# Column halves evicted from tiles of their own, doubled reads, and other layouts for staged weights

## The chip, the cores and the metric

The kernel runs on one core of one Trainium2 chip. Its time is device microseconds (us) from the launch to the end of the last transfer; three runs of the kernel before gave 1161.09 to 1162.67, median 1161.89. A profiled execution is a run of its own, and stands beside these. Engine names are those of the profile: PE (matrix products; PEld its weight loads), DVE, ACT, POOL, SP. DMA transfers are issued by SP (hardware queue q1), a few by ACT (q10), and the adding ones by POOL (software queue q0); all share the core's 16 DMA engines. DMA shares in the profile are means over these 16.

## The reference

Input `x` is 2048 tokens of 576 values, float32. With `xn` its layer norm over the 576 values,

```
out = x + attention(xn @ wqkv) @ wo + relu(xn @ w1) @ w2
```

The attention has 32 heads of 18 values; token s looks at the eight tokens s, s-2, ..., s-14 (those before the start are masked). `w1` is 576 x 4608, `w2` 4608 x 576, `wqkv` 576 x 1728, `wo` 576 x 576. All of it is float32 in and out.

## The kernel before

**Operands.** Each float32 operand of a product is cut in two: a high part, rounded by a copy on ACT, and a low part, the difference, formed on DVE or (for splits marked `pooled`) on POOL (`two`, L170 to L177). A product is then the sum of high x high, high x low and low x high. The 576 rows of a contraction are four pieces of 128 and a last piece of 64. Since a piece of 64 rows fills half of the 128 partitions, it is loaded twice, into partitions 0 to 63 and 64 to 127 (`for part in LOW, UPP`), one DMA for each half.

**Phases.** The tokens are done in two phases `ph` of 1024: eight row blocks of 128, in pairs `tb` of 256 columns of transposed `xn`. In each phase the first six of the 36 column tiles of `w1` (128 columns each) go through plain loops (slots `n`: `h_two` for the hidden layer, `o_two` for its product with `w2`). The other 30 go in 15 pairs `p` by a seven-product (Strassen) scheme: for each pair two groups `g`, one for each two pairs of row blocks; `group` (L1176) runs eight steps, each with a piece of hidden layer, one with `w2` (`o_half`), and one or more evictions.

**The attention** is done in four units `u` of 8 heads (144 columns). The q, k, v products of units 1 to 3 are put into groups 5, 11 and 17 and the group after each; their weights are loaded three groups earlier (`wq_load`, in step 4 of that group, right behind `sw_load` of the next `w1` pair) and split in steps of the next two groups (`wq_split`). The rest of a unit is vector work in a list `bg`, which `run_bg` fills in wherever a small model of DVE's clock (`room`, `DUE`) says that it fits ahead of the next thing that PE waits for.

**Evictions.** A finished PSUM tile is 256 tokens by a column half (`CUT`: 256 or 320 columns). `evict` (L707) copies it on ACT into half of a tile `ev` of 2 x 576 columns; when both halves are there, POOL issues one adding DMA (read the output in HBM, add, write) for each row block of 128 rows, 2304 bytes a row. The pool has two such tiles, so a copy waits until the transfers out of the tile used two pairs earlier have landed. The products with `wo` go the same way, in transfers of 4 x 32 rows. Only the very first sums (phase 0, first three tiles) add `x` on DVE and are stored by SP.

**Queues.** Each engine works in the order in which the code wrote its instructions. SP issues its DMAs in that order too: one that waits for a buffer holds back the ones behind it. SP runs ahead of PE as far as free buffers allow. The pair's `w1` columns come by `sw_load` (L894): four DMAs of two 128 x 128 blocks (512 bytes a row) and two for the last 64 rows; POOL forms sums of them (`sw_mix`), ACT and DVE split them (`sw_prep`).

**Between phases** (the seam) SP writes the attention's transposed output to HBM (`o_out`, L616, eight DMAs a unit), reads it back by token quarters (`ot_in`, by `words_in`, L393), and reads the next phase's transposed `xn` (`xt_in`, also by `words_in`, from `words`). `wo` is staged in HBM and read at the end of a phase (`wo_load`, L254).

Of the kernel before, what the change touches and what calls it, by code (L numbers as in the profile page):

```python
# [26 lines left out]
NU = 4  # L27
# [43 lines left out]
def tile_body(ctx: ExitStack, tc: tile.TileContext, x, wqkv, wo, w1, w2, out):  # L71
# [37 lines left out]
    f32 = lambda ap: ap.bitcast(F32)  # L109

# [74 lines left out]
    def w1_load(ph, c, f):  # L185
# [6 lines left out]
        for part in LOW, UPP:  # L192
            nc.sync.dma_start(st[part, 512:640], w1[KT * P : D, cs])
# [24 lines left out]
    def wq_load(ph, u):  # L218
# [7 lines left out]
        for kt in range(KT + 1):  # L226
            v = z[:, kt, :].rearrange("p (s c) -> p s c", s=3)
            if kt < KT:
                nc.sync.dma_start(v, wq_src[kt * P : (kt + 1) * P, :, c])
            else:  # L230
                for part in LOW, UPP:
                    nc.sync.dma_start(v[part], wq_src[KT * P : D, :, c])
# [310 lines left out]
    def attention(ph, u):  # L543
# [9 lines left out]
        if u == 0:  # L553
            OD[ph] = odp.tile([D, 4, 2 * P], F32, name="od")
# [106 lines left out]
    def ot_in(ph, r):  # L661
# [5 lines left out]
        words_in(f32(lo), OD[ph][:, r])  # L667
# [38 lines left out]

    def evict(ph, tb, h, z, what):  # L707
        key = ph, tb, what
        if key not in EV:
            EV[key] = evp.tile([P, 2, D], F32, name="ev"), []  # L710
        acc, done = EV[key]
        cols = CUT[h]
        nc.scalar.activation(acc[:, :, cols], z[:, :, 0 : cols.stop - cols.start], AF.Copy)  # L713
        done.append(h)
        if len(done) == 2:
            del EV[key]
            for k in range(2):
                if what == "wo":
# [863 lines left out]
```

## Time and profile before

| | |
|---|---|
| median of three runs | 1161.89 us |
| profiled execution, its time | 1158.69 us |
| its span, first to last instruction | 1156.9 us |
| granted clock of PE, mean | 0.994 |
| DMA packets, data | 159811, 176.82 MB |
| DMAs issued by POOL that add (ev and pr) | 276 of 288 KB |

The page cuts the span into 40 slices of 28.9 us with the busy tenths of each engine. A row of the waits names the engine and line that waited, what ended the wait, the total, how often, and the longest. A row of the timeline gives start, duration, engine, line, operation and tiles, and in brackets the idle time just before it with what ended it. A row of the windows gives the stretch, its length, the busy time of each engine with instructions in brackets, the granted clock, the mean busy share of the 16 DMA engines (waiting inside a packet counts, so it can pass 1), and GB/s.

### The profile page before, as it was taken

Reading aid. Unit: us, or ns where it says so; the run is one execution under the profiler, and the core shown is the slowest. Engines: PE = TensorE matmul, PEld = TensorE weight load, DVE = VectorE, ACT = ScalarE, POOL = GpSimd, SP = SyncE. Lnnn points to the kernel's source line nnn. Section 1 sums busy time; section 2 is a strip of 40 time slices with the busy share of each in tenths; the row PEclk is TensorE's granted clock in tenths of the full one; section 3 lists DMA queues with packets and bytes.
Section 4 is the critical chain, followed back from the end, with each engine's and each line's share of the span. In section 5 each row is a group of like instructions: output and inputs, shape, how many; then the busy total and the mean of one; then the engine's idle time right before and its main releaser. Section 6 shows DMA issues by size and latency. Waiting matters only on the chain.

```text
span 1156.9 us, 38381 instructions
## 1 busy us (share of the span) xinstructions
PE 1116.8 (97%) x16410; PEld 1094.4 (95%) x16410; DVE 814.3 (70%) x1249; ACT 560.3 (48%) x1348; POOL 469.5 (41%) x514
## 2 busy tenths in 40 slices
PE   8999999999999999997999999999999999999896
PEld 8999999999999989997999999999999999999895
DVE  7676889699688677964317248868897896888521
ACT  4444464454454455564534345535545544555540
POOL 2324552453353345553322235435524523555331
PEclk9999999999999999998999999999999999999998
DMA  7469985795786687899947258759848957888984
GB/s 219 153 160 218 189 157 93 157 202 89 162 179 122 136 168 140 145 193 267 180 71 164 43 122 171 126 104 191 160 85 179 194 91 170 144 155 141 236 125 112
DMA packets 159811, 176.82 MB, mean 153 GB/s; under 512 B 36233, under 2 KB 107145, under 8 KB 159609
## 3 DMA queue, kind: packets, MB, share of 16 engines
q0 software_dynamic: 44352, 81.45, 46.8%
q1 hardware_dynamic: 114604, 92.03, 27.3%
q8 instruction: 129, 2.11, 0.7%
q10 hardware_dynamic: 684, 0.88, 0.2%
q14 instruction: 42, 0.34, 0.1%
HBM read 74.07 MB, written 95.70 MB: 147 GB/s over the span
## 4 chain that ended last, share of the span: by engine, by line
PE 74%; DMA 10%; DVE 5%; ACT 4%; issue 3%; POOL 1%; SPq 1%; ACTq 0%; DVEq 0%; POOLq 0%
PE po L163 23%; PE po L142 19%; PE ph L163 12%; PE pm L163 9%; PE pm L142 5%; DMA out<-ev 4%; PE ph L142 3%; DMA att<-od 2%; ACT ev L713 1%; PE ph L130 1%; DVE ar L759 1%; DVE ar L176 1%; PE po L130 1%; DVE wq L176 1%; DMA xS<-out 1%
## 5 line engine op out<-in xcount | busy, mean ns | idle before, releaser
L163 PE MATMUL po<-ar 64*128 64x320 f32 (+1 forms) x5760 | 469.2, 291 | 1.5 <-ACT ev L713 1.0
L163 PEld LDWEIGHTS po<-ar 64*128 64x128 f32 x5760 | 410.3, 185 | 4.1 <-ACT ev L713 1.6
L726 POOL DMA_DIRECT2D out<-ev x256 | 226.2, 1024 | 386.6 <-ACT ev L713 346.7
L163 PE MATMUL ph<-xT,ar 64*128 64x256 f32 x2520 | 323.5, 277 | 10.0 <-ACT pm L977 7.2
L163 PEld LDWEIGHTS ph<-xT,ar 64*128 64x128 f32 x2520 | 287.4, 185 | 15.5 <-ACT pm L977 10.3
L713 ACT ACTIVATE ev<-po 128x512 f32<-128x512 f32 (+1 forms) x266 | 171.5, 650 | 219.1 <-PE po L163 95.9
L163 PE MATMUL pm<-xS,ar 64*128 64x256 f32 x2160 | 261.1, 276 | 1.3 <-ACT u L981 0.6
L163 PEld LDWEIGHTS pm<-xS,ar 64*128 64x128 f32 x2160 | 236.9, 184 | 2.9 <-ACT u L981 1.3
L176 DVE TENSOR_TENSOR ar<-st,ar 128x256 fp32r<-128x256 f32 (+3 forms) x232 | 148.8, 646 | 87.5 <-ACT ar L172 76.4
L174 POOL TENSOR_TENSOR ar<-st,ar 128x256 fp32r<-128x256 f32 (+1 forms) x72 | 95.8, 1335 | 160.5 <-ACT ar L172 157.6
L172 ACT ACTIVATE ar<-st 128x256 fp32r<-128x256 f32 (+3 forms) x304 | 148.6, 503 | 15.2 <-DMA st<-in_w 11.5
L909 POOL TENSOR_TENSOR st<-st 128x256 f32<-128x256 f32 x120 | 130.0, 1096 | 12.1 <-DMA st<-in_w 7.7
L142 PE MATMUL po<-wq,xT 64*128 64x432 f32 x1296 | 134.0, 353 | 0.0
L142 PEld LDWEIGHTS po<-wq,xT 64*128 64x128 f32 x1296 | 120.2, 184 | 2.6
L163 PE MATMUL ph<-xS,ar 64*128 64x256 f32 x720 | 104.5, 278 | 9.5 <-ACT ph L977 9.1
L163 PEld LDWEIGHTS ph<-xS,ar 64*128 64x128 f32 x720 | 94.6, 186 | 12.6 <-ACT ph L977 11.8
L599 DVE TENSOR_TENSOR pr<-att 128x1152 f32<-128x1152 f32 x64 | 87.5, 1380 | 0.4
L564 DVE TENSOR_TENSOR pr<-att 128x1152 f32<-128x1152 f32 x64 | 86.4, 1351 | 0.2
L567 DVE TENSOR_REDUCE att<-pr 128x64 f32<-128x1152 f32 x64 | 85.2, 1339 | 0.0
L759 DVE SCALAR_TENSOR_TENSOR ar<-u,ar 128x256 fp32r<-128x256 f32 x60 | 29.8, 497 | 68.5 <-ACT ar L755 68.4
L606 DVE TENSOR_TENSOR pr<-pr 128x1152 f32<-128x1152 f32 x64 | 73.4, 1147 | 1.7
L142 PE MATMUL po<-ar 64*128 64x256 f32 (+1 forms) x984 | 71.0, 289 | 0.0
(121 smaller groups left out, 1360.8 us busy)
## 6 DMA issues: line engine op xcount, KB each, us to landing
out<-ev POOLq DMA_DIRECT2D x266, 288.0 KB, 6.0
st<-in_w SPq DMA_DIRECT2D x72, 288.0 KB
st<-in_w SPq DMA_DIRECT2D x120, 128.0 KB
att<-att SPq DMA_DIRECT2D x16, 441.0 KB
att<-in_wqkv SPq DMA_DIRECT2D x28, 216.0 KB
od<-att SPq DMA_DIRECT2D x32, 128.0 KB
att<-in_x SPq DMA_DIRECT2D x14, 288.0 KB
st<-in_w SPq DMA_DIRECT2D x60, 64.0 KB
```

The source lines that it names most:

```text
L142: ins = nc.tensor.matmul(o, l[z], r[z], start=start, stop=stop)
L163: b.ins = nc.tensor.matmul(b.ap, l[part], r[part], start=start, stop=stop, skip_group_check=skip)
L172: nc.scalar.activation(hi, src, AF.Copy)
L174: nc.gpsimd.tensor_tensor(lo, src, f32(hi), op=ALU.subtract)
L176: nc.vector.tensor_tensor(lo, src, f32(hi), op=ALU.subtract)
L564: nc.vector.tensor_tensor(pr[i], q, window(k, i), op=ALU.mult)
L567: nc.vector.tensor_reduce(lg[:, i], pr.pop(i).rearrange(heads, d=Dh), axis=AX.X, op=ALU.add)
L599: nc.vector.tensor_tensor(pr[i].rearrange(heads, d=Dh), e, window(v, i).rearrange(heads, d=Dh), op=ALU.mult)
L606: nc.vector.tensor_tensor(o, z[:, :, 0:n], z[:, :, n : 2 * n], op=ALU.add)
L713: nc.scalar.activation(acc[:, :, cols], z[:, :, 0 : cols.stop - cols.start], AF.Copy)
L726: ADDED[ph, 2 * tb + k] = nc.gpsimd.dma_start(o_v[ph, 2 * tb + k], acc[:, k, :], accum_op=ALU.add)
L909: nc.gpsimd.tensor_tensor(stg(o), stg(a), stg(b), op=op)
```

## The change

**Evictions.** Each column half has a tile of its own (`ev0` of 2 x 256 columns, `ev1` of 2 x 320, two of each, the same space). When the half has been copied, POOL issues one adding DMA for both row blocks: 256 rows of 1024 or 1280 bytes, where there were two of 128 rows of 2304 bytes for both halves together. For the products with `wo` there are four DMAs instead of two. The first sums are stored by half as well.

**Doubled reads.** The last 64 rows are read by one DMA whose source is `twice(...)`: an access pattern with a leading dimension of 2 and step 0, onto all 128 partitions. So it is in `w1_load`, `wq_load`, `sw_load` (there as two, one for each column tile) and `words_in`.

**Layouts.** `sw_load` reads two row pieces of 256 columns in one DMA (1024 bytes a row), two DMAs instead of four; the staging tile is laid out to fit. The attention's output in HBM holds five blocks of 32 rows for each unit and token quarter, written by one DMA for each quarter (four a unit instead of eight); `ot_in` takes the first four blocks of each unit as a piece of 128 rows and gathers the last piece from 4 units x 16 rows. `wo` is read in the same order, its last piece as 4 x 16 rows.

**Order.** Two places of the split weights are exchanged, the first split of each unit's weights moves from step 3 to step 4, and the second due time of `DUE` is 0.6 us earlier.

What SP issues ahead of unit 1 (`st` rows of 128 columns are `w1` pieces, `st_` with a number a tile of `w2`, `in_wqkv` the unit's weights), before:

```order
L897 DMA st<-in_w 128x2x128 x4
L902 DMA st<-in_w 64x256 x2
L229 DMA att<-in_wqkv 128x3x144 x4
L232 DMA att<-in_wqkv 64x3x144 x2
L207 DMA st_2796<-in_w 128x576
L207 DMA st_2828<-in_w 128x576
```

and now:

```order
L891 DMA st<-in_w 128x2x256 x2
L896 DMA st<-in_w 128x1x128 x2
L229 DMA att<-in_wqkv 128x3x144 x4
L231 DMA att<-in_wqkv 128x3x144
L207 DMA st_2794<-in_w 128x576
L207 DMA st_2826<-in_w 128x576
```

The place in the queue is the same; L896 and L231 are the doubled reads, and the loads of `w2` stand behind them. On SP there are 552 DMAs before and 436 now.

DVE in group 3, before (`st_2301` is `w2`, `wq` the unit's weights, L567 and L564 attention work, L759 the low part of a hidden tile out of PSUM tile `pm`):

```order
L564 TENSOR_TENSOR pr<-att 128x1152
L567 TENSOR_REDUCE att<-pr 128x64
L176 TENSOR_TENSOR ar<-st_2301,ar 128x320
L176 TENSOR_TENSOR wq<-att,wq 128x432
L759 SCALAR_TENSOR_TENSOR ar<-pm,ar 128x256
L176 TENSOR_TENSOR ar<-st,ar 128x256
```

and now:

```order
L562 TENSOR_TENSOR pr<-att 128x1152
L177 TENSOR_TENSOR ar<-st_2299,ar 128x320
L751 SCALAR_TENSOR_TENSOR ar<-pm,ar 128x256
L177 TENSOR_TENSOR ar<-st,ar 128x256
L177 TENSOR_TENSOR wq<-att,wq 128x432
L565 TENSOR_REDUCE att<-pr 128x64
```

A reduction and the unit's first low part went behind the read of `pm`.

POOL in groups 2 and 3, before (L909 the sums of `sw_mix`, `ar<-st_` pooled splits of `w2`):

```order
L726 DMA out<-ev 128x576 x2
L909 TENSOR_TENSOR st<-st 128x256 x3
L726 DMA out<-ev 128x576 x2
L909 TENSOR_TENSOR st<-st 128x256
L726 DMA out<-ev 128x576 x2
```

and now:

```order
L709 DMA out<-ev_2654 128x2x256
L903 TENSOR_TENSOR st<-st 128x2x128 x2
L709 DMA out<-ev_2721 128x2x320
L903 TENSOR_TENSOR st<-st 128x2x128
L709 DMA out<-ev_2789 128x2x256
L709 DMA out<-ev_2856 128x2x320
```

The adding DMA of a first half went ahead of sums that stood before the pair; their number stays, but for `wo`. PE's order is the same row for row.

```diff
 MAT = (
-    dict(A11=5, S1=6, S2=7, A12=8, S3=0, S4=1, A22=2, rem0=3, rem1=4),
-    dict(A11=0, S1=1, S2=2, A12=3, S3=5, S4=6, A22=7, rem0=8, rem1=9),
+    dict(A11=5, S1=6, A12=7, S2=8, S3=0, S4=1, A22=2, rem0=3, rem1=4),
+    dict(A11=0, S1=1, A12=2, S2=3, S3=5, S4=6, A22=7, rem0=8, rem1=9),
 )
-STG = dict(A11=0, S1=1, S2=2, A12=3, S3=4, S4=5, A22=6, rem=7)
+STG = dict(A11=(0, 0), S3=(0, 1), S1=(1, 0), S4=(1, 1), A12=(2, 0), A22=(2, 1), S2=(3, 0), rem=(3, 1))
...
+    twice = lambda ap: ap[None].to_broadcast([2, *ap.shape])
...
     def w1_load(ph, c, f):
...
-        for part in LOW, UPP:
-            nc.sync.dma_start(st[part, 512:640], w1[KT * P : D, cs])
+        nc.sync.dma_start(st[:, 512:640], twice(w1[KT * P : D, cs]))
...
     def wq_load(ph, u):
...
-                for part in LOW, UPP:
-                    nc.sync.dma_start(v[part], wq_src[KT * P : D, :, c])
+                nc.sync.dma_start(v, twice(wq_src[KT * P : D, :, c]))
...
     def wo_load(ph, kt):
...
-            nc.sync.dma_start(lo, wo2[kt * P : (kt + 1) * P, :])
+            nc.sync.dma_start(lo, wo2[kt * UD : kt * UD + P, :])
         else:
             for part in LOW, UPP:
-                nc.sync.dma_start(lo[part], wo2[KT * P : D, :])
+                nc.sync.dma_start(lo[part], wo2.rearrange("(u r) c -> u r c", u=NU)[:, P:UD])
...
     def words_in(z, td):
...
-        for part in LOW, UPP:
-            nc.sync.dma_start(z[part, KT], td[KT * P : D])
+        nc.sync.dma_start(z[:, KT], twice(td[KT * P : D]))
...
-            OD[ph] = odp.tile([D, 4, 2 * P], F32, name="od")
+            OD[ph] = odp.tile([NU, 4, 5, 32, 2 * P], F32, name="od")
...
         def o_out():
-            z = pr.pop("o")
-            f = u * UD
+            z = pr.pop("o").rearrange("p g i e -> p g (i e)")
             for r in range(4):
-                nc.sync.dma_start(
-                    OD[ph][f : f + P, r].rearrange("(g j) t -> j g t", j=32),
-                    z[32 * r : 32 * r + 32, 0:4].rearrange("j g i e -> j g (i e)"),
-                )
-                nc.sync.dma_start(
-                    OD[ph][f + P : f + UD, r], z[32 * r + 16 : 32 * r + 32, 4].rearrange("j i e -> j (i e)")
-                )
+                nc.sync.dma_start(OD[ph][u, r].rearrange("g j t -> j g t"), z[32 * r : 32 * r + 32])
...
     def ot_in(ph, r):
...
-        words_in(f32(lo), OD[ph][:, r])
+        z, od = f32(lo), OD[ph][:, r]
+        nc.sync.dma_start(z[:, 0:KT], od[:, 0:4].rearrange("u g j t -> (g j) u t"))
+        for part in LOW, UPP:
+            nc.sync.dma_start(z[part, KT], od[:, 4, 16:32])
...
+    def ev_tile(h):
+        return evp.tile([P, 2, CUT[h].stop - CUT[h].start], F32, name="ev%d" % h)
+
     def evict(ph, tb, h, z, what):
-        key = ph, tb, what
-        if key not in EV:
-            EV[key] = evp.tile([P, 2, D], F32, name="ev"), []
-        acc, done = EV[key]
         cols = CUT[h]
-        nc.scalar.activation(acc[:, :, cols], z[:, :, 0 : cols.stop - cols.start], AF.Copy)
-        done.append(h)
-        if len(done) == 2:
-            del EV[key]
-            for k in range(2):
...
-                    ADDED[ph, 2 * tb + k] = nc.gpsimd.dma_start(o_v[ph, 2 * tb + k], acc[:, k, :], accum_op=ALU.add)
+        acc = EV[ph, tb, what][:, :, cols] if (ph, tb, what) in EV else ev_tile(h)
+        nc.scalar.activation(acc, z[:, :, 0 : cols.stop - cols.start], AF.Copy)
+        if what == "o":
+            ADDED[ph, tb, h] = nc.gpsimd.dma_start(
+                o_v[ph, 2 * tb : 2 * tb + 2, :, cols].rearrange("i p c -> p i c"), acc, accum_op=ALU.add
+            )
+            return
+        for k in range(2):
+            ins = nc.gpsimd.dma_start(
+                o_v[ph, 4 * k : 4 * k + 4, 32 * tb : 32 * tb + 32, cols], acc[:, k, :], accum_op=ALU.add
+            )
...
     def sw_load(ph, p):
         f = (NC0 * C + 2 * p) * P
-        for name, i, j in (("A11", 0, 0), ("S3", 1, 0), ("A22", 1, 1), ("A12", 0, 1)):
+        for j, r in enumerate((0, 2)):
             nc.sync.dma_start(
-                stg(name).rearrange("p (k c) -> p k c", k=2),
-                w1[2 * j * P : 2 * (j + 1) * P, f + i * P : f + (i + 1) * P].rearrange("(k p) c -> p k c", p=P),
+                ST[:, 512 * r : 512 * (r + 1)].rearrange("p (k c) -> p k c", k=2),
+                w1[2 * j * P : 2 * (j + 1) * P, f : f + 2 * P].rearrange("(k p) c -> p k c", p=P),
             )
-        for part in LOW, UPP:
-            nc.sync.dma_start(stg("rem")[part], w1[KT * P : D, f : f + 2 * P])
+        for i in range(2):
+            nc.sync.dma_start(stg("rem")[:, i, :], twice(w1[KT * P : D, f + i * P : f + (i + 1) * P]))
...
-            for kt, (d, i) in enumerate(((-2, 3), (-2, 7), (-1, 1), (-1, 4), (-1, 6))):
+            for kt, (d, i) in enumerate(((-2, 4), (-2, 7), (-1, 1), (-1, 4), (-1, 6))):
...
-    DUE = (1.0, 3 * STEP + 1.6, 7 * STEP + 1.7, 8 * STEP + 1.0)
+    DUE = (1.0, 3 * STEP + 1.0, 7 * STEP + 1.7, 8 * STEP + 1.0)
```

More of the change, by code (lines that the diff above doesn't have):

```diff
@@ L867, in o_out @@
         t["dve"] = max(t["dve"], t["pe"] - 0.4)
-        key = ph, tb, "o"
-        if key not in EV:
-            EV[key] = evp.tile([P, 2, D], F32, name="ev"), []
-        acc, done = EV[key]
         for k, h in order:
             i, cols = 2 * tb + k, CUT[h]
-            nc.vector.tensor_tensor(acc[:, k, cols], PO[k, h], X[ph, i][:, cols], op=ALU.add)
+            if (tb, h) not in XO:
+                XO[tb, h] = ev_tile(h), []
+            acc, done = XO[tb, h]
+            nc.vector.tensor_tensor(acc[:, k, :], PO[k, h], X[ph, i][:, cols], op=ALU.add)
             dve(cols.stop - cols.start)
             done.append(k)
-            if done.count(k) == 2:
-                at(max(n + 1, BASE[ph] + FIRST), nc.sync.dma_start, o_v[ph, i], acc[:, k, :])
-        if len(done) == 4:
-            del EV[key]
+            if len(done) == 2:
+                to = o_v[ph, 2 * tb : 2 * tb + 2, :, cols].rearrange("i p c -> p i c")
+                at(max(n + 1, BASE[ph] + FIRST), nc.sync.dma_start, to, acc)
     def mat(ph, name):
@@ L1242, in wo_third @@
     def wo_third():
-        EV[0, 3, "wo"] = prp.tile([P, 2, D], F32, name="pr"), []
+        EV[0, 3, "wo"] = prp.tile([P, 2, D], F32, name="pr")
         wo_block(0, 3)
@@ L1322, in epilogue @@
                 ins = nc.sync.dma_start(z[:, r, k], last_rows(2 + r, k, slice(0, D)))
-                for i in range(4 * k, 4 * k + 4):
-                    tc.add_manual_dep(ins.ins, ADDED[1, i].ins.name, SYNC, reason="sums")
+                for tb in 2 * k, 2 * k + 1:
+                    for h in range(2):
+                        tc.add_manual_dep(ins.ins, ADDED[1, tb, h].ins.name, SYNC, reason="sums")
         wo_block(1, 1)
```

35 lines of the change are left out of this document (16 added, 19 removed).

## The prediction

> **What bounds the kernel now.** I read first the page, then what PE waited for, then the timeline at its long waits, then the DMA load by stretches.
>
> ```profile
> span 1156.9 us, 38381 instructions
> PE 1116.8 (97%) x16410; PEld 1094.4 (95%) x16410; DVE 814.3 (70%) x1249; ACT 560.3 (48%) x1348; POOL 469.5 (41%) x514
> PE ph L163 <- ACT ph L977: 9.1, 6, 3.8
> PE ph L163 <- ACT pm L977: 7.2, 12, 0.9
> PE ph L142 <- ACT xT L422: 2.2, 1, 2.2
> PE ph L163 <- ACT ar L172: 1.2, 1, 1.2
> ```
>
> PE is the bound: it is busy for all but 40.1 of 1156.9 us, and its order of work is not changed. So the change can win no more than these idle 40 us, of which the four waits shown hold 19.7. It can lose without limit, wherever something that PE needs comes later. Two kinds of wait are at stake. The first is DVE's order in group 3, and the same in other groups:
>
> ```profile
> 147.66 1.13 DVE L176 TENSOR_TENSOR wq<-att,wq 128x432 fp32r<-128x432 f32 x1
> 148.71 0.41 DVE L759 SCALAR_TENSOR_TENSOR ar<-pm,ar 128x256 fp32r<-128x256 f32 x1
> 149.22 0.37 ACT L977 ACTIVATE pm<-ph 128x256 f32<-128x256 f32 x1 [2.62 <-DVE ar L759]
> 149.64 0.38 PE L163 MATMUL ph<-xT,ar 64*128 64x256 f32 x1 [0.89 <-ACT pm L977]
> ```
>
> PE waits for the copy L977 on ACT, that for the low part L759, which stands on DVE behind two splits (the second of them the unit's weights). The second kind is the eviction, in the seam and at the end of phase 1:
>
> ```profile
> 523.18 0.74 ACT L674 ACTIVATE att<-att 128x640 fp32r<-128x640 f32 x1 [2.53 <-DMA att<-od]
> 525.75 0.60 ACT L713 ACTIVATE ev<-po 128x512 f32<-128x512 f32 x1 [1.83 <-DMA out<-ev]
> 528.22 0.38 PE L163 MATMUL ph<-xS,ar 64*128 64x256 f32 x1 [3.78 <-ACT ph L977]
> 1094.72 0.60 ACT L713 ACTIVATE ev<-po 128x512 f32<-128x512 f32 x1 [3.47 <-DMA out<-ev]
> 1097.18 0.38 PE L163 MATMUL ph<-xS,ar 64*128 64x256 f32 x1 [2.77 <-ACT ph L977]
> ```
>
> ACT stands at a copy into `ev` until an earlier transfer has landed (1.83 and 3.47 us), and the copy L977 behind it comes late. What sets both are the DMA engines:
>
> ```profile
> q0 software_dynamic: 44352, 81.45, 46.8%
> q1 hardware_dynamic: 114604, 92.03, 27.3%
> core 0: us, PE busy (x) PEld busy (x) DVE busy (x) ACT busy (x) POOL busy (x), PEclk, DMA share, GB/s
> 125.00:136.00 11.00, 11.00 (x186) 11.00 (x185) 8.61 (x14) 6.73 (x17) 6.63 (x8) 1.00 0.97 185
> 136.00:142.00 6.00, 6.00 (x102) 6.00 (x101) 5.13 (x7) 2.13 (x5) 3.25 (x4) 1.00 1.07 235
> 142.00:150.00 8.00, 7.11 (x115) 6.84 (x113) 6.91 (x10) 4.67 (x13) 4.76 (x6) 1.00 1.11 242
> 150.00:161.00 11.00, 11.00 (x187) 11.00 (x184) 10.14 (x17) 8.39 (x22) 5.51 (x6) 1.00 0.71 130
> 515.00:530.00 15.00, 11.22 (x171) 10.84 (x169) 7.86 (x16) 9.23 (x21) 5.43 (x8) 0.97 1.08 266
> 530.00:545.00 15.00, 12.40 (x166) 11.56 (x164) 3.69 (x8) 7.23 (x18) 5.77 (x6) 0.92 1.07 258
> ```
>
> On the mean they are 75% busy (46.8 + 27.3, and 1.0 in three small queues). But while a unit's weights are loaded (125 to 150) and in the seam the share stands at 0.97 to 1.11: full. The same load comes six times, ahead of units 1 to 3 of both phases.
>
> **The gains.** *Order of DVE.* A reduction and the 432-column split leave the path ahead of L759. The rows give at most 7.2 us (twelve waits); I take 5, since the waits without a first piece of weights keep their cause. *Evictions.* The transfer of a first half leaves one half earlier, and its tile is free that much sooner, so I count the ACT wait as gone: 1.8 of the 3.8 us in the seam (the rest belongs to L674, which waited 2.53 us for the attention's output), all 2.8 at 1097, and half of what is left of the 9.1, so 6 of at most 9.1. *Fewer issues.* The 1.2 us wait is for a load of `w2` that SP issued behind eight writes of `od`; now there are four: 1.2. Together 12.2 us.
>
> **Parts with little on the path.** The `w1` blocks come in half as many rows, twice as long: same bytes, taken at 0. The copies on ACT have the same sizes. The adding transfers:
>
> ```profile
> out<-ev POOLq DMA_DIRECT2D x266, 288.0 KB, 6.0
> L726 POOL DMA_DIRECT2D out<-ev x256: 592/897/1224, 79.7 to 1110.7; - x128
> ```
>
> Their bytes stay, their rows double (33,800 more). No row shows an adding row of 1 KB. At the plain queue's time for a packet (27.3% x 16 x 1156.9 us / 114604 = 44 ns) they cost 93 us on each engine, 8% of the span; by bytes alone nothing; at the 195 ns that an adding packet has now (46.8%, 44352 packets), 412 us or 36%. The adding queue moves 9.4 bytes a ns and the plain one 18.2, half, as reading and writing back would make it, so I take the 8%: hidden on the mean (75 to 83%), felt where the engines are full. POOL's issue, 0.90 us (median) for 128 rows, may double: 276 x 0.9 = 0.25 ms at most, on an engine that is 41% busy and waits mostly for evictions; taken at 0.
>
> **The doubled reads.** Here I expect the loss. The last stores of the kernel show what the first dimension of a list of rows does:
>
> ```profile
> 1127.19 10.75 DMA xS<-out
> xS<-out SPq DMA_DIRECT2D x4, 288.0 KB
> 1148.00:1150.00 2.00, 0.00 (x0) 0.00 (x0) 0.00 (x0) 0.00 (x0) 0.00 (x0) 1.00 0.26 100
> ```
>
> After 1148 only the last stores are in flight; their side in HBM is 4 x 32 rows, and the share is 0.26: four of 16 engines, with 100 GB/s together, some 24 GB/s each. The four reads `xS<-out`, also 4 x 32 rows, took 10.75 us for 1.18 MB, 110 GB/s, the same again. A doubled read begins with a dimension of 2, so by the same behaviour it runs on two engines, at about 48 GB/s: 1.4 us for 64 KB (a `w1` piece), 2.7 for the 128 KB of `xT`, 4.6 for the 216 KB of a unit's last weights. The Trainium skill ("DMA: Bandwidth & Descriptors", on why a DMA increments its semaphore by 16) states this as a rule, with a leading broadcast of c copies held to c engines; the stores above agree for 4, and no run here shows it for 2.
>
> *A unit's loads.* The queue, and the first reader of the `w2` tile that stands last in it:
>
> ```profile
> 130.26 5.23 SPq L897 DMA_DIRECT2D st<-in_w  x4
> 137.13 2.98 SPq L229 DMA_DIRECT2D att<-in_wqkv  x4
> 140.16 1.29 SPq L232 DMA_DIRECT2D att<-in_wqkv  x2
> 141.54 6.57 SPq L207 DMA_DIRECT2D st<-in_w  x2
> 156.69 0.92 ACT L172 ACTIVATE ar<-st 128x256 fp32r<-128x256 f32 x2
> ```
>
> Two pieces of `w1` and the last weights put 1.4 + 1.4 + 4.6 = 7.4 us on two engines, less the 0.9 that their sixteenths cost now: 6.5 more, in a stretch that is full until 150. From 150 on 0.29 is free: 1.9 us until 156.7. So the `w2` tile is some 4.6 us late, ACT stops at its split, and PE with it once the PSUM tiles are full. I take 4 us for each of the six loads, 24; the bounds are 0 (if the engines' other work gives way) and 7.4. In groups without such a load the 2.8 us for a pair fit into the free 0.29.
>
> *The seam.*
>
> ```profile
> 543.08 0.31 ACT L426 ACTIVATE xT<-xT 64x128 fp32r<-64x128 f32 x1 [2.19 <-DMA xT<-words]
> 544.29 0.38 PE L142 MATMUL ph<-xT,ar 64*128 64x256 f32 x1 [2.23 <-ACT xT L422]
> 546.00:549.50 3.50, 3.50 (x32) 3.33 (x32) 2.13 (x5) 2.31 (x5) 1.76 (x2) 0.51 1.12 298
> ```
>
> L426 is the split of `xT`'s last piece, and it already waits 2.19 us for it; PE starts behind it, and the half clock at 546 (0.51) is that wait's echo. Now three pieces of `w1` (4.2) and its own read (2.7) lie on two full engines: 6.9 us, and 1 to 2 for the last pieces of `od` and `wo`, 4 x 16 rows, on four; SP has four writes of `od` less to issue, some 2 us at half of L232's 1.29 each. I take 7; bounds 0 and 14 (when adding transfers share each engine by halves). *The head.*
>
> ```profile
> 10.08 0.74 ACT L172 ACTIVATE ar<-st 128x640 fp32r<-128x640 f32 x1 [0.24 <-DMA st<-in_w]
> ```
>
> The third piece of `w1` was already waited for (0.24 us). Three doubled reads put 4.2 us on two engines, SP issues three DMAs less (0.65 each, as L232's two): 1 us, bounds 0 and 3. *The end.* The last sum's read, its products and the stores keep their order; one issue of 0.9 us is off it, and the adding rows are shorter: 0.
>
> **Sum.** 24 + 7 + 1 - 12.2 = 19.8, taken as 20 us. The profiled execution's own time is 1158.69, so 1178.7; it lies 3.2 under the median, to which I add the same: 1182.
>
> **Rivals.** *1, faster.* The doubled reads don't hurt: they are spread over all engines, or two engines catch up before the first reader. Then the gains stand alone, 1161.9 - 12 = 1150. For it: 15 us lie between the issue of that `w2` load and its reader, and SP has 116 DMAs less to issue. Against it: it decides at 6.5 us of free time on two engines in those 15, and the rows leave 1.9. The Trainium skill has a rule on this side too (same page, rules for kernel authors): two transfers to the two halves of the partitions run one behind the other anyway, better one of 128 partitions. *2, nearly even.* Units are absorbed, the seam isn't: 1161.9 - 12 + 8 = 1158. *3, the adding rows.* If a row costs nearer to 195 ns than to 44, the engines pass 75 + 36 = 111% and the kernel waits for them throughout: halfway, at 97%, every group is as full as the stretch before 150; I put it at 1210.
>
> **Chances.** The forecast 0.56 (its own range 1166 to 1204), rival 1 0.25, rival 2 0.11, rival 3 0.08. From no change a measurement tells about 0.2%, 2.3 us: faster 0.30 (rival 1 and half of rival 2), same 0.06, slower 0.64. The range goes from 1149, the middle of rival 1, to 1204; half of rival 1 and the upper ends are left out.
>
> **What would show it.** Two rows of ACT's waits are the measure:
>
> ```profile
> ACT ev L713 <- DMA out<-ev: 54.5, 20, 3.8
> ACT ar L172 <- DMA st<-in_w: 11.5, 6, 4.3
> ```
>
> Right: ACT waits for DMAs into `st` (L172) rise from 11.5 us in all to 20 or more, and PE waits behind them ahead of units 1 to 3; the `xT` wait near 543 grows; waits of ACT for `out<-ev` fall from 54.5 us to under 20; PE's 7.2 us for `pm` fall to 2. Wrong: the DMA share ahead of a unit's products stays with no wait of ACT behind it, or the adding queue's share goes beyond 60%.

## The result and the profile after

The changed kernel takes 1224.49 us (median of four runs, 1223.15 to 1226.39), the kernel before beside it 1161.49 (1159.78 to 1162.67): a ratio of 1.0545, 95% interval 1.0524 to 1.0565. It is 63 us slower, where the prediction had 20 and a range that ended at 1204.

The page of the changed kernel (its span, the busy time of the engines, the two large DMA queues with packets, MB and share of 16 engines):

```profile
span 1224.6 us, 38252 instructions
PE 1144.1 (93%) x16410; PEld 1119.1 (91%) x16410; DVE 856.1 (70%) x1249; ACT 563.3 (46%) x1348; POOL 560.2 (46%) x526
q0 software_dynamic: 84480, 81.49, 49.7%
q1 hardware_dynamic: 101348, 92.54, 26.4%
```

Of the 67.7 us that the span grew, PE is busy for 27.3 more (1144.1 against 1116.8, for the same 16410 products) and idle for 40.4 more. The adding queue has 84480 packets instead of 44352, and took 49.7% of the span, 609 us of each engine, instead of 541. What PE waited for (total us, times, longest):

```profile
PE ph L164 <- ACT ar L173: 28.0, 8, 4.1
PE ph L164 <- ACT ph L971: 9.9, 2, 5.4
PE ph L164 <- ACT pm L971: 6.6, 12, 2.0
PE po L143 <- ACT ev L707: 6.4, 3, 5.9
PE ph L143 <- ACT xT L420: 5.9, 1, 5.9
```

And what ACT waited for from DMAs:

```profile
ACT ar L173 <- DMA st<-in_w: 73.6, 17, 11.7
ACT att L668 <- DMA att<-od: 12.6, 3, 6.5
ACT xT L420 <- DMA xT<-words: 4.7, 1, 4.7
```

The wait for a split of `w2` (L173, L172 before) rose from 1.2 us to 28.0; ACT in turn waits 73.6 us for loads into `st`, 11.5 before. The 54.5 us that ACT waited for `out<-ev` are gone, and nothing of it shows in the time. The largest of the new waits come ahead of units 1 to 3, six times. The first, in the timeline (start, duration, engine, what, and in brackets the idle time before with its releaser):

```profile
144.87 11.25 SPq L207 DMA_DIRECT2D st<-in_w  x2
164.02 0.94 ACT L173 ACTIVATE ar<-st 128x256 fp32r<-128x256 f32 x2 [6.82 <-DMA st<-in_w]
165.01 0.58 PE L164 MATMUL ph<-xT,ar 64*128 64x256 f32 x1 [4.13 <-ACT ar L173]
```

SP stands for 11.25 us at its two loads of `w2` (10.2 of them at the first), ACT gets the first one's tile late (the semaphore that it waits for is that load's), and PE stops for 4.13 us. The six stops last 4.13, 4.00, 4.12, 4.08, 3.65 and 3.67 us. What the DMA engines do during the first (stretch and length, busy us of PE, PEld, DVE, ACT, POOL, granted clock, DMA share, GB/s):

```profile
160.00:161.00 1.00, 0.88 (x16) 0.69 (x14) 0.00 (x0) 0.00 (x0) 0.00 (x0) 1.00 1.09 292
161.00:162.00 1.00, 0.00 (x0) 0.00 (x0) 0.00 (x0) 0.00 (x0) 0.00 (x0) 1.00 0.28 68
162.00:163.00 1.00, 0.00 (x0) 0.00 (x0) 0.00 (x0) 0.00 (x0) 0.00 (x0) 1.00 0.15 40
163.00:164.00 1.00, 0.00 (x0) 0.00 (x0) 0.00 (x0) 0.00 (x0) 0.00 (x0) 0.74 0.13 51
```

While PE stands, the share falls to 0.15 and 0.13, which is about two engines of 16. The packets of the trace tell what these two carry. Of the 256 rows of the two `w2` tiles, 224 (14 sixteenths) have been read by 160; the other 32, two sixteenths, follow only from 162.58 on, as the rows of the unit's weights run out (the last at 162.97). The other stops look alike: two of 16 parts wait in four of them, at shares of 0.13 to 0.17, and one part in the last, at 0.07.

Then follows what the prediction left out, in the second of these stretches:

```profile
150.00:161.00 11.00, 10.88 (x179) 10.58 (x176) 8.68 (x14) 5.84 (x15) 3.61 (x3) 1.00 0.98 185
163.50:170.30 6.80, 5.25 (x40) 4.95 (x42) 5.22 (x7) 4.48 (x11) 4.78 (x4) 0.50 0.55 102
170.30:177.00 6.70, 6.70 (x108) 6.70 (x106) 3.33 (x6) 3.09 (x8) 3.95 (x4) 1.00 1.01 156
```

For 6.8 us the granted clock is 0.50. Such stretches stand behind eleven stops, 61.2 us in all, where before had two of 3.4 us. At half clock half of it is lost: (61.2 - 6.8) / 2 = 27.2 us, the whole growth of PE's busy time (27.3).

PE's order is the same, so the start of each product can be set against the start of the same product before. By how much the distance grew in each stage (us, stages by the time of before; the kernels below the first row are the experiments). Each row rests on one profiled execution of each kernel, and such a one can lie some 3 us off: that of before is 2.8 us under its median, that with all doubled reads undone 3.7 over.

```
                                 to 100  100-450   450-640  640-1040  1040-1140  rest   span
                                         units     seam     units     end
the changed kernel                  1.3     16.5      22.2      21.5        4.8    1.4   67.7
unit reads undone                   2.7     -3.5      22.2      -1.5        7.7    1.0   28.6
all doubled reads undone            0.0     -2.8       6.2      -0.8        8.1    2.8   13.5
... and gather of 16 x 4 rows      -0.2     -3.3       0.3      -1.0       -0.9    1.5   -3.5
... and evictions of before         0.0     -4.8      -1.0      -3.9        3.3    0.0   -6.6
evictions alone, on before         -0.2     -0.8      -0.4       2.2       -0.6    2.5    2.7
```

### The profile page after: what moved, and what is told of

It reads as the page before. It is cut to its first block, busy times and chain, and to the rows that moved or that the text cites. A ratio compares the mean times of both kernels' runs of the same rounds, so it can differ in the third digit from the quotient of the medians.

```text
span 1224.6 us, 38252 instructions
## 1 busy us (share of the span) xinstructions
PE 1144.1 (93%) x16410; PEld 1119.1 (91%) x16410; DVE 856.1 (70%) x1249; ACT 563.3 (46%) x1348; POOL 560.2 (46%) x526
## 3 DMA queue, kind: packets, MB, share of 16 engines
q0 software_dynamic: 84480, 81.49, 49.7%
## 4 chain that ended last, share of the span: by engine, by line
PE 68%; DMA 16%; DVE 8%; ACT 3%; SPq 3%; issue 2%; ACTq 0%; DVEq 0%
PE po L164 21%; PE po L143 19%; DMA st<-in_w 11%; PE ph L164 11%; PE pm L164 8%; PE pm L143 4%; PE ph L143 3%; DMA att<-od 2%; DVE ar L177 2%; DVE ar L751 2%; DVE pr L562 1%; DMA od<-att 1%; DMA xT<-words 1%; ACT ar L173 1%; SPq L229 1%
## 5 line engine op out<-in xcount | busy, mean ns | idle before, releaser
L709 POOL DMA_DIRECT2D out<-ev x256 | 305.2, 1212 | 404.5 <-ACT ev L707 170.7
L164 PE MATMUL po<-ar 64*128 64x320 f32 (+1 forms) x5760 | 476.7, 295 | 2.1 <-ACT ev L707 1.3
L164 PEld LDWEIGHTS po<-ar 64*128 64x128 f32 x5760 | 416.4, 189 | 6.1 <-ACT ev L707 1.9
L164 PE MATMUL ph<-xT,ar 64*128 64x256 f32 x2520 | 335.8, 282 | 38.3 <-ACT ar L173 28.0
L164 PEld LDWEIGHTS ph<-xT,ar 64*128 64x128 f32 x2520 | 296.0, 189 | 47.6 <-ACT ar L173 29.6
L164 PE MATMUL pm<-xS,ar 64*128 64x256 f32 x2160 | 272.1, 281 | 1.3 <-DVE u L980 0.4
L164 PEld LDWEIGHTS pm<-xS,ar 64*128 64x128 f32 x2160 | 244.2, 188 | 2.9 <-issue 0.9
L177 DVE TENSOR_TENSOR ar<-st,ar 128x256 fp32r<-128x256 f32 (+3 forms) x232 | 155.3, 673 | 115.8 <-ACT ar L173 106.0
L173 ACT ACTIVATE ar<-st 128x256 fp32r<-128x256 f32 (+3 forms) x304 | 148.6, 502 | 77.6 <-DMA st<-in_w 73.6
L175 POOL TENSOR_TENSOR ar<-st,ar 128x256 fp32r<-128x256 f32 (+1 forms) x72 | 89.9, 1252 | 132.1 <-ACT ar L173 130.5
L164 PEld LDWEIGHTS ph<-xS,ar 64*128 64x128 f32 x720 | 97.0, 189 | 11.2 <-ACT ph L971 10.4
L562 DVE TENSOR_TENSOR pr<-att 128x1152 f32<-128x1152 f32 x64 | 93.9, 1468 | 0.2
L597 DVE TENSOR_TENSOR pr<-att 128x1152 f32<-128x1152 f32 x64 | 89.8, 1418 | 0.7
L143 PEld LDWEIGHTS po<-ar 64*128 64x128 f32 x984 | 67.6, 188 | 6.3 <-ACT ev L707 6.1
```

The source lines that it names most:

```text
L143: ins = nc.tensor.matmul(o, l[z], r[z], start=start, stop=stop)
L164: b.ins = nc.tensor.matmul(b.ap, l[part], r[part], start=start, stop=stop, skip_group_check=skip)
L173: nc.scalar.activation(hi, src, AF.Copy)
L175: nc.gpsimd.tensor_tensor(lo, src, f32(hi), op=ALU.subtract)
L177: nc.vector.tensor_tensor(lo, src, f32(hi), op=ALU.subtract)
L562: nc.vector.tensor_tensor(pr[i], q, window(k, i), op=ALU.mult)
```

## The experiments

**All doubled reads undone.** The changed kernel with two DMAs of 64 rows again at every place.

```diff
-        nc.sync.dma_start(z[:, KT], twice(td[KT * P : D]))
+        for part in LOW, UPP:
+            nc.sync.dma_start(z[part, KT], td[KT * P : D])
...
```

> The changed kernel with every doubled read undone: the last 64 rows come again by two DMAs of 64 rows each, all other parts of the change stay. Theory (doubled reads run on two engines, PE waits behind them, and each wait is followed by a stretch of half clock): the six waits of some 4 us ahead of units 1 to 3 and the long ones of the seam go, and so do the half clock stretches, so 1145 to 1162 us. Rival (the doubled rows of the adding transfers and POOL's longer issue are the cause): at least 1190 us, with the 4 us waits still there.

Measured: 1168.55 us, ratio 1.0049 (1.0032 to 1.0065), above the expected 1162. So 56 of the 63 us are the doubled reads'. But the rest of the change, counted as 12 us of gain, costs 0.5%.

**What is it in a doubled read?** Two kernels read as many bytes with one DMA each: 128 following rows (leading dimension 128), or two blocks of 64 rows that lie apart (leading dimension 2, its step not 0). In both a half of the last piece holds other rows of the same array, so the sums are not the reference's.

```diff
-        nc.sync.dma_start(st[:, 512:640], twice(w1[KT * P : D, cs]))
+        nc.sync.dma_start(st[:, 512:640], w1[KT * P - 64 : D, cs])
...
```

> The changed kernel in which each doubled read takes 128 following rows (the last 64 and the 64 ahead of them) instead of the last 64 twice: the same number of DMAs, the same bytes and places in SBUF, no step of 0, and a first dimension of 128. The lower half of the last piece then holds other rows, so the sums differ from the reference's. Theory (the first dimension of the source sets the number of engines): as if spread over all 16, 1140 to 1160 us. Rival (one DMA of 128 partitions in place of two costs it, or SP's order): stays near 1224.

```diff
+    apart = lambda ap: (
+        ap.rearrange("(b r) s c -> b r s c", r=64) if len(ap.shape) == 3 else ap.rearrange("(b r) c -> b r c", r=64)
+    )[0:5:4]
...
-        nc.sync.dma_start(st[:, 512:640], twice(w1[KT * P : D, cs]))
+        nc.sync.dma_start(st[:, 512:640], apart(w1[2 * P : D, cs]))
...
```

> The changed kernel in which each doubled read takes two different blocks of 64 rows (rows 256 to 319 and 512 to 575): a first dimension of 2 with a step that is not 0, nothing read twice. The lower half of the last piece then holds other rows, so the sums differ from the reference's. Theory (first dimension of 2, whatever its step, means two engines): within 1% of the changed kernel, 1212 to 1236 us. Rival (reading the same rows twice in one DMA is what is slow): like 128 following rows, 1140 to 1165.

Measured: 1166.29 us (ratio 1.0037, 1.0019 to 1.0056; 6 us above the theory's range, as the kernel with paired reads was) and 1225.73 (1.0542, 1.0497 to 1.0587). That the same rows are read twice does not matter; the leading dimension of 2 does. The same shows in how long SP stood at the 72 loads of `w2` that come behind such reads (min/median/max ns), in before, in the changed kernel and in these two:

```profile
L207 SPq DMA_DIRECT2D st<-in_w x72: 327/376/1543, 7.5 to 1081.3; - x72
```

```profile
L207 SPq DMA_DIRECT2D st<-in_w x72: 328/462/11363, 7.2 to 1146.1; - x72
```

```profile
L207 SPq DMA_DIRECT2D st<-in_w x72: 327/358/2787, 5.2 to 1085.8; - x72
```

```profile
L209 SPq DMA_DIRECT2D st<-in_w x72: 328/524/11139, 7.4 to 1141.0; - x72
```

An issue that takes 0.4 us takes up to 11 us behind reads with a leading 2. No record says what SP waits for there; that the two engines still have such reads to do is the explanation that fits all four. Both kernels saved as many issues as the changed one, and the kernel of 128 rows was only 2.3 us faster than the one with paired reads, with intervals that overlap: fewer DMAs on SP were worth little.

**Doubled reads alone, on the kernel before.**

```diff
-        for part in LOW, UPP:
-            nc.sync.dma_start(stg("rem")[part], w1[KT * P : D, f : f + 2 * P])
+        nc.sync.dma_start(stg("rem"), twice(w1[KT * P : D, f : f + 2 * P]))
...
```

> The kernel before with the doubled reads alone (all five places, also the reads of the attention's output, eight more than in the changed kernel). Theory: the whole loss is in them, 1205 to 1245 us, with six waits of 3 to 6 us ahead of units 1 to 3. Rival (they hurt only together with the doubled rows of the adding transfers, which fill the engines): 1165 to 1185.

Measured: 1212.35 us, 1.0427 (1.0406 to 1.0448), some 50 us. The theory's range holds, but not its stops of 3 to 6 us: those ahead of the units were shorter than in the changed kernel (up to 2.2 us in the trace), and the loss with them. The seam alone lost 22.6.

**Which doubled reads?** First the changed kernel with those of the unit's last weights undone.

```diff
-                nc.sync.dma_start(v, twice(wq_src[KT * P : D, :, c]))
+                for part in LOW, UPP:
+                    nc.sync.dma_start(v[part], wq_src[KT * P : D, :, c])
```

> The changed kernel (1224.5 us) with the doubled read of the units' last weights alone undone (two DMAs of 64 rows again); all other doubled reads stay. Theory: the 216 KB on two engines are what carries the six stalls of PE (23.7 us in all), since the two w1 pieces alone (2.8 us) fit into what is left free; with the stalls go the stretches of half clock behind them (30.6 us at half, so 15.3): 1224.5 - 39 = 1185.5, between 1180 and 1195. Rival: the two w1 pieces of a pair are enough to make the w2 tile late, and the stalls stay, shorter: 1205 to 1224. If the half clock is not the stalls' consequence, only 23.7 come back: 1201.

Measured: 1187.81 us, 1.0227 (1.0196 to 1.0257). All six stops are gone, and 36.7 us with them: more than the 23.7 of the stops, near the 39 of stops and half clock. Then the opposite, with the unit reads as the only doubled ones, on the kernel with the gather of the next experiment (1156.94 us):

```diff
-                for part in LOW, UPP:
-                    nc.sync.dma_start(v[part], wq_src[KT * P : D, :, c])
+                nc.sync.dma_start(v, twice(wq_src[KT * P : D, :, c]))
```

> The kernel with all doubled reads undone and the gather across units (1156.9 us), with one doubled read put back: that of a unit's last weights, 216 KB, at six places. The prediction's own working, by bytes on two engines: 4.6 us less the 0.6 that it cost before and the 1.9 that are free, so stalls of 2.1 us and half of 3.4 us at half clock behind each: 1156.9 + 6 x 3.8 = 1180. Rival, the whole read lies on the path: the six stalls are as long as in the changed kernel (3.7 to 4.1 us) with their half clock, so the step from paired to doubled reads costs the same 36.7 us as there: 1190 to 1196.

Measured: 1160.66 us, 1.0002 (0.9984 to 1.0020). Both expectations missed: 3.7 us, not 23 or 37. The trace tells why. SP still stands at the load, and ACT reads the tile without waiting:

```profile
L208 SPq DMA_DIRECT2D st<-in_w x72: 327/462/8851, 7.5 to 1087.1; - x72
155.51 0.93 ACT L173 ACTIVATE ar<-st 128x256 fp32r<-128x256 f32 x2
```

Of six such places one made PE stop (1.68 us). The prediction left 1.9 us free between the load and its reader; the slack is larger. In the kernel before, the rows of the first `w2` tile have been read by 148.9, and its reader starts at 156.69, 7.8 us later. Holds of SP of 6.8 to 8.9 us at these loads are just absorbed; in the changed kernel, with the two `w1` pieces of the pair on the same engines, five are 10.2 to 11.4 us (the sixth is 8.1, behind another 8.1 at the unit's own loads), and PE stops for about 4.

**The reads of `xT` alone**, on the same kernel.

```diff
-        for part in LOW, UPP:
-            nc.sync.dma_start(z[part, KT], td[KT * P : D])
+        nc.sync.dma_start(z[:, KT], twice(td[KT * P : D]))
```

> The same kernel (1156.9 us), with the doubled read of the last piece of xT alone put back (128 KB, four in a phase). The prediction's working: its own 2.7 us on two engines less the 0.4 of sixteen are 2.3 at the one wait in the seam, and up to 3.4 more at half clock: 1159 to 1163. Rival, this read is what makes the seam 15 us longer in the kernel with the unit reads paired: 1168 or more.

Measured: 1167.37 us, 1.0055 (1.0033 to 1.0078): 10.4 us, between the two and close to the rival. The wait is not at the reader of `xT`:

```profile
549.77 9.35 SPq L397 DMA_DIRECT2D xT<-words  x1
569.97 0.78 ACT L173 ACTIVATE ar<-st 128x256 fp32r<-128x256 f32 x2 [14.46 <-DMA st<-in_w]
571.28 0.58 PE L143 MATMUL po<-ar 64*128 64x256 f32 x2 [8.66 <-ACT ev L709]
```

SP stands 9.35 us at the last doubled read, and the load of `w2` queued behind comes so late that ACT waits 14.46 us for it and PE 8.66. In the changed kernel it is the same place:

```profile
583.82 8.71 SPq L207 DMA_DIRECT2D st<-in_w  x1
600.38 0.77 ACT L173 ACTIVATE ar<-st 128x256 fp32r<-128x256 f32 x2 [11.69 <-DMA st<-in_w]
601.69 0.58 PE L143 MATMUL po<-ar 64*128 64x256 f32 x2 [5.89 <-ACT ev L707]
```

**Does the half clock follow the stop?** The kernel before, with idle copies on ACT ahead of one copy into `ph` in eight groups without unit loads.

```diff
+        for _ in range(LATER.get((ph, g), 0) if to == "q" else 0):
+            nc.scalar.activation(idle, ident, AF.Copy)
...
```

> The kernel before (1161.5 us), with idle copies on ACT (128x128, some 0.25 to 0.3 us each, into a tile that nothing reads) ahead of the first copy into ph in eight groups that load no unit: 4, 6, 8 and 10 of them in groups 7, 8, 13 and 14 of phase 0, and 13, 16, 20 and 26 in the same groups of phase 1. So PE stalls there by about 1 to 8 us less what ACT has in hand, with the DMA load, the reads and the order as before. Theory, the half clock follows the stall: behind every stall of some 2 us and more stands a stretch of 3.4 or 6.8 us at a granted clock of 0.5, behind the shorter ones none; the eight stalls come to some 24 us and cost 30 to 38: 1190 to 1200. Rival, the half clock comes from what full DMA engines or the seam do: no stretch at half clock behind any of the eight, and the time rises by the stalls alone: 1180 to 1188.

Measured: 1195.14 us, 1.0296 (1.0266 to 1.0326), in the range of the theory. The stops, and the 10.2 us behind each of them:

```profile
227.65 0.38 PE L164 MATMUL ph<-xS,ar 64*128 64x256 f32 x1 [1.64 <-ACT ph L986]
324.65 0.58 PE L164 MATMUL ph<-xS,ar 64*128 64x256 f32 x1 [2.19 <-ACT ph L986]
792.36 0.58 PE L164 MATMUL ph<-xS,ar 64*128 64x256 f32 x1 [2.95 <-ACT ph L986]
810.23 0.58 PE L164 MATMUL ph<-xS,ar 64*128 64x256 f32 x1 [4.35 <-ACT ph L986]
921.98 0.58 PE L164 MATMUL ph<-xS,ar 64*128 64x256 f32 x1 [7.76 <-ACT ph L986]
```

```profile
227.64:237.84 10.20, 10.19 (x168) 10.19 (x170) 7.46 (x9) 5.26 (x13) 6.37 (x8) 1.00 0.76 176
324.66:334.86 10.20, 10.20 (x143) 10.20 (x145) 7.47 (x9) 4.64 (x11) 4.08 (x6) 0.83 0.76 178
792.36:802.56 10.20, 10.20 (x144) 10.20 (x146) 8.64 (x12) 4.85 (x12) 4.01 (x5) 0.84 0.56 106
810.23:820.43 10.20, 10.20 (x122) 10.20 (x124) 6.72 (x8) 4.64 (x11) 3.60 (x5) 0.71 0.74 170
921.98:932.18 10.20, 10.20 (x144) 10.20 (x146) 7.54 (x9) 4.63 (x11) 4.82 (x7) 0.83 0.73 170
```

Of these eight places one has no stop and one a stop of 1.24 us. Behind that and behind 1.64 us the clock stays at 1.00; behind the stops of 2.19 us and more there is a stretch at half. Set against the same products before, up to 12 us behind each, the stops of 1.64, 2.19, 2.95, 4.35, 5.33 and 7.76 us cost 1.6, 4.2, 4.6, 7.2, 7.4 and 9.7. The longest two pay less extra than that of 4.35 since their half clock begins earlier inside the stop.

The length of a stop alone does not decide, though. In the kernel with the unit reads alone doubled, 3.4 us at half follow the stop of 1.68 us, and in the kernel before none follow the stop of 2.77 us at 1097. All traces together show what does. In each of the 15 the granted clock changes only at marks 3.41 us apart. Away from the head and the tail of the kernel they have 66 changes to half. In the 3.41 us ahead of each, PE was idle for 1.62 us or more in all; where the clock stayed full behind such a stretch, PE had been idle in it for 1.91 us at most. So the half clock follows where PE stands for about half of a stretch between two marks. The stop of 2.77 us was cut by a mark, with no more than 1.61 us of idle time on either side.

The DMA share behind the forced stops is 0.56 to 0.76, so full engines are not needed for it. The Trainium skill ("TensorE: Matmul & The Clock Gate", HAM oscillation — how this bites in real kernels) warns of idle gaps over some 3.4 us. Here 1.62 us of idle time between two marks were enough, and the measurement decides.

**The missing gains.** The kernel without doubled reads still lost 6.2 us in the seam and 8.1 at the end of its profiled execution. At the end the timeline shows:

```profile
1090.48 4.57 SPq L664 DMA_DIRECT2D att<-od  x2
1102.86 0.74 ACT L671 ACTIVATE att<-att 128x640 fp32r<-128x640 f32 x1 [7.60 <-DMA att<-od]
1105.95 0.58 PE L164 MATMUL ph<-xS,ar 64*128 64x256 f32 x1 [7.65 <-ACT ph L976]
```

ACT waits 7.60 us for `od`, and SP stands at reads of its last piece, 4 units x 16 rows. So the next kernel takes these rows, and those of `wo`, in another order, 16 rows x 4 units; both operands of the product change alike.

```diff
-            nc.sync.dma_start(z[part, KT], od[:, 4, 16:32])
+            nc.sync.dma_start(z[part, KT], od[:, 4, 16:32].rearrange("u j t -> j u t"))
...
-                nc.sync.dma_start(lo[part], wo2.rearrange("(u r) c -> u r c", u=NU)[:, P:UD])
+                nc.sync.dma_start(lo[part], wo2.rearrange("(u r) c -> r u c", u=NU)[P:UD])
```

> The kernel with every doubled read undone (1168.6 us), with one edit: the last pieces of od and wo are gathered row by row across the four units (leading dimension 16, then 4), where it read 4 units of 16 rows (leading dimension 4). Both operands take the same new order, so the sums are the same. Theory, four engines: a read with a leading dimension of 4 runs on four engines, and that is what holds back L671 by 7.6 us at the end of phase 1 and 4.9 in the seam. Then the 8.6 us that PE loses at the end, some 2.4 of the seam and a part of the 2.8 behind the last product come back: 1155 to 1159. Rival, adding rows: the doubled adding rows load all engines, the order of the gather does not matter: 1166 to 1171.

Measured: 1156.94 us, 0.9967 (0.9948 to 0.9985). The bytes, the rows and the count of DMAs are the same; the leading dimension went from 4 to 16, and 11.6 us came back (9.5 by the two ratios): the waits of ACT for `od` are gone. The Trainium skill ("DMA: Bandwidth & Descriptors", on why a DMA increments its semaphore by 16) gives a DMA as many engines, up to 16, as divide its slowest dimension. The times for 2, 4, 16 and 128 agree with it, and for 2 the shares of 0.13 to 0.17 at the stops.

The rival, adding rows, was tried beside it, on the kernel with the late reads of `od`:

```diff
-        if what == "o":
-            ADDED[ph, tb, h] = nc.gpsimd.dma_start(
-                o_v[ph, 2 * tb : 2 * tb + 2, :, cols].rearrange("i p c -> p i c"), acc, accum_op=ALU.add
-            )
...
+                else:
+                    ADDED[ph, 2 * tb + k] = nc.gpsimd.dma_start(o_v[ph, 2 * tb + k], acc[:, k, :], accum_op=ALU.add)
```

> The kernel with every doubled read undone (1168.6 us), with the evictions of before: one tile of 2 x 576 columns, adding transfers of 128 rows of 2304 bytes once both halves are there, first sums stored by row block. Theory, four engines: the reads of od and wo stay as they are, so the end and the seam stay late; what the halves gained is lost, 0 to 3 us: 1167 to 1172. Rival, adding rows: without the doubled rows and with half of POOL's issue time the lost 8.6 us at the end and the seam come back: 1155 to 1160.

Measured: 1167.77 us, 1.0051 (1.0032 to 1.0070), against 1168.55: nothing. But here ACT's late copies behind `od` (PE stops of 9.3 and 9.4 us at 519.5 and 1092.6) may cover what the evictions do. With the gather put right, the same edit:

> The kernel with all doubled reads undone and the gather across units (1156.9 us), with the evictions of before (whole rows of 2304 bytes, 128 to a transfer, once both halves are there). Theory from the runs so far: evictions by halves bring nothing that can be measured and their doubled rows cost nothing: 1154 to 1160. Rival, the prediction's gain: the halves were worth 6 us, hidden so far behind the late reads of od: 1161 to 1165.

Measured: 1151.05 us, 0.9911 (0.9891 to 0.9931), the fastest of all, faster than both kernels. ACT waits longer than ever for a free tile, and PE is busy for 1115.6 us:

```profile
ACT ev L710 <- DMA out<-ev: 73.9, 32, 4.0
PE 1115.6 (97%) x16410; PEld 1098.6 (95%) x16410; DVE 816.1 (71%) x1249; ACT 560.7 (49%) x1348; POOL 473.5 (41%) x514
```

Both theories missed: whole-row evictions were 5.9 us better. Since the two stood beside different runs of before, the evictions were then tried alone: the kernel before with the edit the other way round, the changed kernel's `evict`, its tiles and its stores of the first sums.

> The kernel before (1161.5 us) with the evictions of the changed kernel alone: a tile for each column half, one adding transfer for two row blocks, first sums stored by half. Theory from the last runs: the halves cost some 6 us (1156.9 with them, 1151.1 without): 1165 to 1169. Rival, the prediction's term: waits of ACT for a free tile go, 6 us gained: 1153 to 1157. Third, nothing either way, and the 6 us between those two kernels hang on what else they hold: 1159 to 1163.

Measured: 1163.27 us, 1.0020 (1.0004 to 1.0037): a cost of some 2 us, not a gain of 6, a little above the range of the third expectation. Its page:

```profile
PE 1116.9 (96%) x16410; PEld 1092.8 (94%) x16410; DVE 852.5 (74%) x1249; ACT 563.6 (49%) x1348; POOL 565.4 (49%) x526
q0 software_dynamic: 84480, 81.49, 52.9%
L715 POOL DMA_DIRECT2D out<-ev x256 | 306.9, 1218 | 405.8 <-ACT ev L713 174.0
```

POOL issues 80 us longer (306.9 us in the group, 226.2 before), and DVE is busy for 852.5 us, 814.3 before, with the same 1249 instructions. The low parts of the hidden tiles, 25 of these 38 us, show where (min/median/max ns; `m` lies in SBUF, `pm` in PSUM). Before:

```profile
L759 DVE SCALAR_TENSOR_TENSOR ar<-m,ar x60: 411/418/965, 120.5 to 1107.3; 128x256 fp32r<-128x256 f32 x60
```

and with the evictions alone:

```profile
L757 DVE SCALAR_TENSOR_TENSOR ar<-m,ar x60: 415/425/1900, 120.3 to 1108.0; 128x256 fp32r<-128x256 f32 x60
L757 DVE SCALAR_TENSOR_TENSOR ar<-pm,ar x72: 384/412/425, 15.8 to 1109.9; 128x256 fp32r<-128x256 f32 x72
PE ph L163 <- ACT pm L974: 9.6, 17, 0.9
```

Of the 60 out of `m`, the 32 that run beside an adding issue alone take 0.42 us on the mean, as with POOL idle; the 26 that meet POOL's arithmetic take 1.83, all of the long ones beside sums of `sw_mix` (before, 14 meet POOL's arithmetic and take 0.92). Low parts out of PSUM are never slower than 0.43 us. So it is not the longer issue that slows DVE: the adding DMA of a first half now goes ahead of sums, and these run later, just when DVE makes the low part out of SBUF. PE's waits for `pm` are 9.6 us, 7.2 before. The difference is as large as the cost, but whether the one makes the other was not tried. Last, the order alone:

```diff
-            for kt, (d, i) in enumerate(((-2, 3), (-2, 7), (-1, 1), (-1, 4), (-1, 6))):
+            for kt, (d, i) in enumerate(((-2, 4), (-2, 7), (-1, 1), (-1, 4), (-1, 6))):
...
-    DUE = (1.0, 3 * STEP + 1.6, 7 * STEP + 1.7, 8 * STEP + 1.0)
+    DUE = (1.0, 3 * STEP + 1.0, 7 * STEP + 1.7, 8 * STEP + 1.0)
```

> The kernel before (1161.5 us) with the change of order alone: the first split of a unit's weights in step 4, and the second due time 0.6 us earlier. Theory: PE's waits for the copy L977 ahead of units go, 0.9 us at each of six places: 1155.5 to 1158.5. Rival: the split and the reduction now delay other work on DVE, and the gain is given back: 1161 to 1164.

Measured: 1158.64 us, 0.9965 (0.9944 to 0.9986), a gain of 4.1 us by the ratio, just above the theory's range. The wait that it was meant for went, from 7.2 us:

```profile
PE ph L163 <- ACT pm L977: 0.9, 4, 0.2
```

## Why the prediction was right and wrong

The sign, the cause and the place of the largest loss were right: leading dimension 2, two engines, `w2`'s tile late ahead of units 1 to 3. By differences of medians the 63 us are: unit reads 36.7, the other doubled reads 19.2, the gather of 4 x 16 rows 11.6, all else -4.6. The forecast's 19.8 us were all idle time of PE; in the profiled executions idle time grew by 40.4, and the half clock added 27.3 of busy time, for which the sum had no term.

- *"I take 4 us for each of the six loads, 24."* The stops sum to 23.7 us. The step that failed is the next one: the prediction named the half clock as the echo of one wait in the seam, and gave none to the stops that it forecast. Six stretches of 3.4 or 6.8 us, 30.6 in all, cost another 15.3. Over the kernel, seam and end included, this term is 27.2 us, the largest part of the miss.
- *How late, and by which way.* The bytes gave 4.6 us and the stop was 4, and that is luck: two errors cancel. The last 384 rows of the unit's weights (576 bytes each), as many as the doubled read has, took 11.9 us (151.06 to 162.97) and not 4.6: 19 GB/s in place of 48. The sum took the rate of engines that do nothing else, while adding transfers ran on these two as well; how much of the loss is theirs is open. Against that, the tile had 7.8 us in hand and not 1.9, for the reader at 156.69 reads the first `w2` tile and not the last. Nor does the working hold for the unit reads alone: it leaves 2 us of delay, and these cost 0.6 each. What is late is the part of the `w2` tile on the two engines, behind the read, after SP had been held at that load for up to 11.4 us.
- *Seam 7, bounds 0 and 14.* It lost 22.2. The doubled reads make 16 of it (22.2 - 6.2), the stops and their half clock together; the `xT` reads alone cost 10.4 us, by a held load of `w2` and not at their own reader, where the term was placed.
- *"1 to 2 for the last pieces of `od` and `wo`", "the end: 0".* With the end of phase 1 they cost 11.6. The prediction had the rule for a leading 4 and its row, and applied it to the seam's bytes only; SP's hold at the end was not looked for. *The head*: 1 forecast, 1.3 in the trace.
- *Gains 12.2.* Order: 5 forecast, 4.1 measured (1.6 to 6.5). Evictions: 6 forecast, some 2 lost. ACT's 54.5 us of waiting went as foreseen, and lay beside PE's work; with them came 38 us more of DVE time, where DVE and the sums on POOL meet, for which the prediction had no term. That this costs the 2 us is not shown. Fewer issues: not tried alone; with the layouts of staging and `od` they are inside the 5.6 us that the fastest kernel gains beyond the order (1160.70 beside it less 1151.05, less 4.1).
- *Doubled adding rows, rival 3.* 84480 packets instead of 44352 took 67 us more of each engine, where the prediction had 0 to 412 and took 93. With the evictions alone the queue stands at 52.9%, and the kernel pays 0.2%: the rival fell.
- *Rival 1* fell with the kernel of paired reads, which took 56 us off; *rival 2* with the six stops. Of the signs named, three came (ACT's waits for `st` and for `xT` up, those for `out<-ev` gone). PE's 7.2 us for `pm` stayed at 6.6 in place of 2, though the order alone brings them to 0.9; with the evictions by halves and paired reads they are 4.1.

## What to carry to other kernels

Before two DMAs are made one, look at the first dimension of the new access pattern: 2 or 4 in front made reads of the same bytes hold up the whole issuing queue, and putting 16 in front, by an order of rows that both operands share, took 11.6 us off again. A tile is there only when its last part is, and the parts on the engines of such a read wait behind it. A delay on one queue costs nothing up to its slack and comes through beyond it, so price two such parts together and apart. A stop of PE of 2 us and more is to be priced with the half clock that mostly follows it, here 1.6 to 2.9 us on top.

## What was not expected of the hardware

An issue on SP's hardware queue can itself last 11 us, in front of a load that has its buffer free; why is open. The half clock goes by idle time between marks 3.41 us apart, and 1.62 us of it were enough. A DVE instruction of 0.42 us out of SBUF took up to 1.9 us beside a sum on POOL, and 0.42 beside POOL's issue of an adding DMA. And the 40128 more packets of the adding queue cost 67 us on each of 16 engines, 27 ns each, less than the 44 and 195 between which the prediction chose.
